# Attention ahead of two mixture layers: float32 matmuls on halves and quarters of the array in place of split operands

## The chip, the core and the metric

One NeuronCore of one Trainium2 chip runs the whole program in one launch. The metric is device time in microseconds (us), the median of several runs. In the profile PE is TensorE (matmuls), PEld its weight loads, DVE is VectorE, ACT is ScalarE, POOL is GpSimd and SP issues the DMAs.

## The reference, cut to what matters

```python
B, H, S, D = 4, 8, 576, 64              # q, k, v: (4, 8, 576, 64) float32
q_rot, k_rot = rotate(q), rotate(k)      # rotary embedding over halves of D
scores = D ** -0.5 * q_rot @ k_rot.T     # 576 x 576 for each of 32 heads
scores = scores - max(scores, axis=-1)
attn = exp(scores); attn = attn / (sum(attn, axis=-1) + 1e-09)
x = (attn @ v), heads side by side       # 2304 tokens x 512
x = relu(x @ w_in) ** 2 @ w_out          # 512 -> 2048 -> 512
out = top-1 mixture of 8 experts of x    # 512 -> 1024 -> 512 each, scaled by two gates
```

All inputs are float32, and so is the output.

## The kernel before

The 32 heads are taken in 16 pairs (`NP`), two heads j = 0, 1 in the two halves of the 128 partitions. `prepare(p)` loads q and k of a pair, rotates them (a shuffle on VectorE, two products and a sum on GpSimd) and builds the matmul operands; `unit(P, p, c)` takes 128 queries of the pair (c = 0 to 3; c = 4 takes the last 64 queries of both heads together) through scores, least value, exponential and transposes; `values(P, p, g)` multiplies by v once a group of queries is complete (group 0: 256 queries, group 1: 320). q and k carry the sign and scale so that the search is for a minimum.

The kernel does its matmuls in the type `F32R` (float32r in the program), whose products keep fewer bits than float32. So each operand is split into a high part (a copy rounded to `F32R`) and a low part (the value minus its high part), and products of parts are added up in PSUM. In attention that means: `high_k`/`low_k` (tile `hl`) and `high_q`/`low_q` (tile `d`), with two DMAs a head (`fan`) that put k under both halves; `v_high`/`v_low` (`vh`); and for the exponentials (`pt`), once turned by TensorE into `tp`, a high copy `phi` on ScalarE and a low part `plo` on VectorE (`evacuate`). What is left of a row beyond 512 keys has its own PSUM tile, `rem`. `scores` are 4 matmuls of 128x128 by 288 for a head and 128 queries.

The least score of a row is found by a `tensor_reduce` on VectorE straight from PSUM (`least`, L473); `exponential` (L479) then reads the scores from the same PSUM tile with that least value as its bias.

The order of work on each engine is not written by hand. `Plan` gets every step with its engine, a price in ns, its dependencies, the tile slots that it uses (`Ring`) and a key, runs through them once, and emits them in the order of their planned start; a step of low priority (a high key) fills what the others leave open. Two rings matter here: scores have two PSUM tiles (`ps_s`), transposes two (`ps_t`); `rem` and `ov` (the product with v) have one bank each.

Beside attention, `add_conversion` turns the 64-bit copies of w_in and w_out into pages of high and low parts (16 values of f, two half conversions for each: three steps on ScalarE, L740, L720 and L747, and four on VectorE, L728, L733, L743 and the subtraction `pg<-m,pg`). They have the lowest priority in attention and mostly run in the first block behind it. Behind attention come four blocks of 512 tokens and one of 256 through the first layer (L841 and L871), then routing and the experts; these are not touched by the change but for the numbers of the planner.

A step `warm` at the start has TensorE do 24 `F32R` matmuls and some float32 ones on zeros, on half the rows (64*128) and quarters (64*64) of the array, while the first loads run (L280, L283, L292). Its results are not used.

Of the kernel before, what the change touches and what calls it, by code (L numbers as in the profile page):

```python
# [28 lines left out]
HB = S // 2  # L29
GRP = ((0, 256), (256, 320))  # L30
# [3 lines left out]
NF0, NF1 = 2, 4  # L34
# [9 lines left out]
ROPE, SPLIT, TURN, SHIFT = "pppppp", "aapppp", "aaaaaaaaaaaa", "aaaa"  # L44


TAIL, LATE = -25204, -2110543
HI, LO = "aaavaaav", "vpvvvpvv"
DMA_RATE = 241
AHEAD = dict(ACT=225, DVE=15, PE=4, POOL=207, SP=534)  # L50
BEGIN = (4, 6, 6, 1)
SECOND = "ap"
EXPONENT = "a"
KEYS = dict(fan=-1072502, swap=10791310, step=11801431, conv=17070875, x0=6215731, end=10978483, load=-22393304, rope=15947290, qk=10250273, v=2755321, s=-18767946, min=-13921801, exp=2252693, rc=-16180141, t=8460321, hi=331733, lo=-7898202, pv=15728628, x=-132386)
# [143 lines left out]
def two_moe_kernel(ctx, tc, qk, v, tab, cst, w_in, w_out, wg, w1, w2, out):  # L198
# [51 lines left out]
    def add_attention(ctx, rest, first):  # L250
# [4 lines left out]
        ps_1 = pool(ctx, "ps_1", 1, space=PSUM)  # L255
# [3 lines left out]
        tabs = pre.tile([128, 4, S], F32, name="tabs")  # L259
        ring_x, ring_hl, ring_d = plan.ring(2), plan.ring(2), plan.ring(2)  # L260
        ring_vr, ring_vh, ring_xt = plan.ring(1), plan.ring(2), plan.ring(2)
        ring_s, ring_p, ring_t = plan.ring(2), plan.ring(3), plan.ring(2)
        ring_rem, ring_o = plan.ring(1), plan.ring(1)
        ring_h = [plan.ring(1), plan.ring(1)]
        ring_sm, ring_f = plan.ring(2), plan.ring(1)
        sums = [big.tile([128, 9], F32, name=f"sums{i}") for i in range(2)]

        ends_q = big.tile([128, 2, 128], F32R, name="dz")
        ring_z = plan.ring(1)
        zeros = [plan.add("DVE", 150, lambda: ve.memset(f32(ends_q), 0.0), -5000000, [], [])]  # L270
        ready = plan.add("SP", 780, lambda: sp.dma_start(out=ident, in_=cst[:, 0:128]), -5000000, [], [])

        def warm():
            z = ends_q.rearrange("p j q -> p (j q)")
            y = f32(z)
            t = [ps_1.tile([128, 512], F32, tag=t, name=n) for t, n in (("o", "ov"), ("rem", "rem"))]
            half = slice(0, 64), slice(64, 128)

            def rows(h, x, m=128, c=0):
                te.matmul(out=t[h][c:c + m, 0:256], lhsT=x[half[h], 0:m], rhs=x[half[h]], start=True, stop=True)  # L280

            def turn(h, i):
                te.transpose(out=t[h][:, 64 * i:64 * i + 64], in_=y[half[h], 0:128], identity=ident[half[h], half[h]])  # L283

            def quads(x, n):
                for i in range(n):
                    for c in (0, 64):
                        for h in range(2):
                            rows(h, x, 64, c)

            for i in range(24):
                te.matmul(out=t[i % 2][:, 0:256], lhsT=z[:, 0:128], rhs=z, start=True, stop=True)  # L292
            quads(y, 4)
            for i in range(3):
                for h in range(2):
                    rows(h, y)
            for i in range(4):
                for h in range(2):
                    turn(h, i)
            quads(y, 1)  # L300
            for i in range(4):
                for h in range(2):
                    turn(h, i)
            quads(y, 1)

        plan.add("PE", 10000, warm, -5000000, zeros + [ready], [ring_o.take(), ring_rem.take()])

        def prepare(p):
# [4 lines left out]
            xs = ring_x.take()  # L313

            first = p == 0

            def load(i):

                if "x" not in T:
                    T["x"] = pre.tile([128, 4, S], F32, tag="x", name="x", bufs=2)  # L320
                sp.dma_start(out=T["x"][:, 2 * i], in_=qk[p, :, i])
                if first and i:
                    sp.dma_start(out=tabs[:, 2:4], in_=tab)

            def swap(i):
                ve.stream_shuffle(out=T["x"][:, 2 * i + 1], in_=T["x"][:, 2 * i], mask=[j ^ 1 for j in range(32)])  # L326

            def mul(i):
                x = T["x"]
                eng(3 * (i // 2) + i % 2).tensor_tensor(out=x[:, i], in0=x[:, i], in1=tabs[:, i], op=ALU.mult)  # L330

            def add(i):
                x = T["x"]
                eng(3 * i + 2).tensor_tensor(out=x[:, 2 * i], in0=x[:, 2 * i], in1=x[:, 2 * i + 1], op=ALU.add)

            def operand():
                if "d" not in T:
                    T["d"] = two.tile([128, 2, 3, S], F32R, tag="d", name="d")
                return T["d"]

            def high_k():
                T["hl"] = pre.tile([128, 2, S], F32R, tag="hl", name="hl", bufs=2)
                copy(split[1], T["hl"][:, 0], T["x"][:, 2])

            def low_k():
                sub(ve if split[3] == "v" else po, T["hl"][:, 1], T["x"][:, 2], f32(T["hl"][:, 0]))

            def high_q(j, on):
                h = slice(64 * j, 64 * j + 64)
                copy(on, operand()[h, j, 0], T["x"][h, 0])  # L350

            def low_q(j, on):
                h, o = slice(64 * j, 64 * j + 64), slice(64 - 64 * j, 128 - 64 * j)
                sub(ve if on == "v" else po, T["d"][o, j, 0], T["x"][h, 0], f32(T["d"][h, j, 0]))

            def first_high(j, u):
                h, o = slice(64 * j, 64 * j + 64), slice(64 * u, 64 * u + 64)
                se.copy(out=operand()[o, j, 1], in_=T["x"][h, 2])

            def first_low(j, u):  # L360
                h, o = slice(64 * j, 64 * j + 64), slice(64 * u, 64 * u + 64)
                sub(ve, operand()[o, j, 2], T["x"][h, 2], f32(T["d"][h, j, 1]))

            def fan(j):
                h = slice(64 * j, 64 * j + 64)
                for u in (0, 64):
                    sp.dma_start(out=f32(operand()[u:u + 64, j, 1:3]), in_=f32(T["hl"][h]))

            def scale_tables():

                se.activation(out=tabs[:, 0:2], in_=tabs[:, 2:4], func=AF.Copy, scale=-(D ** -0.5))

            on, split = ("vvvvvv", "aavvap") if first else (choice(ROPE, p, 6), choice(SPLIT, p, 6))
            eng = lambda i: ve if on[i] == "v" else po
            price = lambda i: ("DVE", dves(S)) if on[i] == "v" else ("POOL", pool2(S))
            hls, ds = ring_hl.take(), ring_d.take()
            parts = {}
            for i in (1, 0):
                k = key + KEYS["rope"] - i
# [265 lines left out]
        for p in range(NP):  # L645
            P = made.pop(p)
            for c in range(5):
                unit(P, p, c)
# [958 lines left out]
def _shape_constants():  # L1607
# [12 lines left out]
    o = 384  # L1620
# [46 lines left out]
```

## Time and profile before

| | |
|---|---|
| median of 3 runs | 981.05 us (978.38 to 981.15) |
| the profiled execution | 981.04 us, of which 979.3 us are its span |
| PE busy | 934.5 us (95%), 5640 matmuls |
| DVE busy | 662.6 us (68%), 1255 instructions |
| ACT busy | 544.0 us (56%), 1141 instructions |
| POOL busy | 356.9 us (36%), 291 instructions |
| first matmul of the first layer | at 302.2 us |
| clock of TensorE in the span (granted, mean) | 0.985 |

Busy shares are means over stages that differ. Up to some 300 us the program is in attention, and PE, DVE, ACT and POOL are all busy; from there on PE alone is busy nearly throughout. A matmul's busy time includes its way through the array, so that several that follow each other overlap; from the start of one row to the start of the next is what it takes of its engine.

### The profile page before, as it was taken

What the parts mean: (1) busy time and instruction counts of PE and PEld (TensorE: products, weight loads), DVE (VectorE), ACT (ScalarE), POOL (GpSimd) and SP (SyncE); (2) the same over time, 40 slices, a digit from 0 to 9 for tenths busy, and PEclk for the clock granted to TensorE, in tenths of its full rate; (3) what the DMA queues carried; (4) which work ended last, traced back from release to release, by engine and by line L of the source; (5) the groups of instructions that cost most, each with busy time, mean ns of one, the idle gap of its engine ahead of it and who ended that gap; (6) DMA issues with size and microseconds to landing.
All of it is one profiled execution on the core that took longest, in us unless ns stands there. A gap on an engine that the chain in (4) does not pass through costs nothing.

```text
span 979.3 us, 16392 instructions
## 1 busy us (share of the span) xinstructions
PE 934.5 (95%) x5640; PEld 817.6 (83%) x5640; DVE 662.6 (68%) x1255; ACT 544.0 (56%) x1141; POOL 356.9 (36%) x291
## 2 busy tenths in 40 slices
PE   5999999999999999999999999999999899999994
PEld 4898998998897887778777877888998799999993
DVE  7888889899997987542454244353668799367660
ACT  3899999999997786322222223223443464344441
POOL 4899998899962000000000000000131454234440
PEclk8999999999999999999999999999999899999998
DMA  3656874757675661410030002001641512443430
GB/s 119 154 154 178 205 203 132 198 153 205 177 211 178 220 213 54 129 44 1 20 118 26 1 24 74 1 0 34 249 150 45 203 55 78 159 136 136 140 121 18
DMA packets 55704, 115.41 MB, mean 118 GB/s; under 512 B 8992, under 2 KB 18736, under 8 KB 55600
## 3 DMA queue, kind: packets, MB, share of 16 engines
q1 hardware_dynamic: 52480, 104.17, 35.8%
q0 software_dynamic: 3120, 9.96, 3.0%
q8 instruction: 51, 0.84, 0.4%
q14 instruction: 53, 0.43, 0.1%
HBM read 94.24 MB, written 19.21 MB: 116 GB/s over the span
## 4 chain that ended last, share of the span: by engine, by line
PE 64%; DVE 12%; DMA 10%; ACT 7%; POOL 3%; issue 3%; SPq 1%; DVEq 0%; POOLq 0%; ACTq 0%
PE h L841 19%; PE a L871 18%; PE h L1359 8%; PE a L1447 7%; DMA out_dram<-y,sidx 4%; PE sc L458 3%; ACT pt L479 3%; DVE mx L473 3%; PE ov L614 2%; DVE plo L212 2%; PE tp L513 2%; ACT phi L209 2%; DMA pg<-w_dram 1%; DMA x<-qk_dram 1%; DVE x L326 1%
## 5 line engine op out<-in xcount | busy, mean ns | idle before, releaser
L841 PE MATMUL h<-xhi,pg 128*128 128x512 f32 (+1 forms) x640 | 198.9, 374 | 0.0
L871 PE MATMUL a<-gh,pg 128*128 128x512 f32 (+1 forms) x640 | 196.1, 373 | 0.0
L1313 POOL DMA_INDIRECT raw<-x1d,gidx x20 | 20.0, 1000 | 376.7 <-DVE ssc L243 358.2
L848 ACT ACTIVATE r<-h 128x512 f32<-128x512 f32 (+1 forms) x80 | 44.3, 554 | 193.4 <-PE h L841 180.8
L841 PEld LDWEIGHTS h<-xhi,pg 128*128 128x128 f32 x640 | 117.4, 188 | 23.1
L871 PEld LDWEIGHTS a<-gh,pg 128*128 128x128 f32 x640 | 117.2, 188 | 22.1
L856 DVE TENSOR_TENSOR r<-r 128x512 f32<-128x512 f32 (+1 forms) x64 | 40.0, 625 | 124.3 <-ACT gh L852 124.2
L871 PE MATMUL a<-gl,pg 128*128 128x512 f32 (+1 forms) x320 | 119.5, 373 | 1.9 <-DVE gl L212 1.6
L841 PE MATMUL h<-xlo,pg 128*128 128x512 f32 (+1 forms) x320 | 119.0, 372 | 0.0
L473 DVE TENSOR_REDUCE mx<-sc 128x1 f32<-128x576 f32 x144 | 107.1, 750 | 15.3 <-PE sc L458 10.6
L458 PE MATMUL sc<-d 128*128 128x288 f32 x512 | 98.7, 317 | 14.0 <-DVE d L212 10.4
L479 ACT ACTIVATE pt<-sc,mx 128x576 f32<-128x576 f32 x144 | 107.5, 748 | 5.7 <-DVE mx L473 5.1
L1359 PE MATMUL h<-raw,pg 128*128 128x256 f32 x864 | 106.0, 283 | 1.1 <-DVE ht L1368 1.1
L1359 PEld LDWEIGHTS h<-raw,pg 128*128 128x128 f32 x864 | 105.0, 191 | 2.2 <-PE m L911 1.0
L212 DVE TENSOR_TENSOR plo<-tp,phi 128x512 fp32r<-128x512 f32 x144 | 96.3, 682 | 10.8 <-ACT phi L209 9.5
L458 PEld LDWEIGHTS sc<-d 128*128 128x128 f32 x512 | 74.7, 194 | 20.4 <-DVE d L212 11.2
L513 PE MATMUL tp<-ident,pt 128*128 128x128 f32 x576 | 86.2, 275 | 5.0 <-DVE plo L212 4.2
L330 POOL TENSOR_TENSOR x<-x,tabs 128x576 f32<-128x576 f32 x60 | 86.4, 1457 | 7.6 <-DVE x L326 7.3
L209 ACT CAST phi<-tp 128x512 fp32r<-128x512 f32 x144 | 83.1, 586 | 7.3 <-PE tp L513 5.8
L212 DVE TENSOR_TENSOR pg<-pg,pg 128x512 fp32r<-128x512 f32 x90 | 76.0, 872 | 4.3 <-ACT pg L209 4.1
L513 PEld LDWEIGHTS tp<-ident,pt 128*128 128x128 f32 x576 | 68.4, 141 | 7.9 <-issue 2.9
L871 PEld LDWEIGHTS a<-gl,pg 128*128 128x128 f32 x320 | 60.3, 188 | 15.2 <-DVE gl L212 4.5
(236 smaller groups left out, 1743.9 us busy)
## 6 DMA issues: line engine op xcount, KB each, us to landing
pg<-w_dram SPq DMA_DIRECT2D x160, 256.0 KB
d<-hl SPq DMA_DIRECT2D x60, 288.0 KB
x<-qk_dram SPq DMA_DIRECT2D x32, 288.0 KB
xtd<-xt SPq DMA_DIRECT2D x32, 288.0 KB
raw<-w_in_dram SPq DMA_DIRECT2D x16, 512.0 KB
raw<-w_out_dram SPq DMA_DIRECT2D x16, 512.0 KB
vr<-v_dram SPq DMA_DIRECT2D x16, 352.0 KB
x1d<-b SPq DMA_DIRECT2D x18, 256.0 KB
```

The lines of the kernel that those rows point to most:

```text
L209: (ve.tensor_copy if on == "v" else se.copy)(out=out, in_=in_)
L212: eng.tensor_tensor(out=out, in0=a, in1=b, op=ALU.subtract)
L330: eng(3 * (i // 2) + i % 2).tensor_tensor(out=x[:, i], in0=x[:, i], in1=tabs[:, i], op=ALU.mult)
L458: te.matmul(out=t[:, hf, 0:HB], lhsT=ends_q[:, 1] if both else d[:, j, 0, q0 + 64 * j:q0 + 64 * j + n], rhs=d[:, 1 if both else j, part, z ...
L473: ve.tensor_reduce(out=T["mx", j], in_=T["s", j][:, :, 0:HB], axis=AX.XY, op=ALU.min)
L479: se.activation(out=T["pt"][:, j].rearrange("p (a b) -> p a b", a=2), in_=T["s", j][:, :, 0:HB], func=AF.Exp, bias=T["mx", j], scale=-1.0, ...
L513: te.transpose(out=t[:, k], in_=T["pt"][:, j, i:i + 128], identity=ident)
L841: te.matmul(out=G["t"], lhsT=a[:, 128 * c:128 * c + 128], rhs=m[:, c, :n], start=c == 0 and i == 0, stop=c == KC - 1 and i == 2,)
L848: se.activation(out=G["r"], in_=G["t"], func=AF.Relu)
L871: te.matmul(out=T["acc", d][:, :n], lhsT=a[:, 128 * d:128 * d + 128], rhs=m, start=f == 0 and i == 0, stop=f == NF - 1 and i == 2,)
L1359: te.matmul(out=T["t"][:, f], lhsT=m[:, z], rhs=r[:, c], start=i == 0, stop=i == 11)
L1447: te.matmul(out=T["t"], lhsT=a[:, k, 128 * i:128 * i + 128], rhs=m, start=k == 0 and y == 0, stop=k == KF - 1 and y == 2,)
```

## The change

Attention's matmuls run in float32 itself, and nothing in attention is split. One head has 64 rows (D), so a score matmul takes half the array: the two row halves h = 0, 1 multiply at the same time, one for each half of the keys, and write two PSUM banks. k is laid out for this on the host; q of each head is needed in both halves, which two DMAs for a pair (`cross`, tile `c`) provide. The product with v takes quarters of the array (64*64), four at a time; transposes take halves (64*128). When the last step was in quarters, scores are done in quarters as well (`mode`). The exponentials are laid out in blocks of 32 keys of the two heads, so that a turned block of 64 rows holds both.

The least value now comes from a `tensor_scalar` (times 1, minimum into `accum_out`) that also writes the scores to SBUF (`sb`); the exponential reads them there. Turned exponentials are copied once (`pp`), by VectorE or ScalarE as `TURN` says (640 columns on VectorE and 512 on ScalarE for each 128 queries). Transposes, the product with v and the turned sums share two PSUM tiles of two banks (`tp`). The step `warm` is gone; the first pair's rotation stays on VectorE. More pages are placed so that they can be written during attention (`NF0`, `NF1`), and the planner's keys, lookaheads and prices are new. The layer behind attention and the experts have the same instructions, in nearly the same order.

```diff
-NF0, NF1 = 2, 4
+NF0, NF1 = 7, 8
...
-ROPE, SPLIT, TURN, SHIFT = "pppppp", "aapppp", "aaaaaaaaaaaa", "aaaa"
+ROPE, TURN, SHIFT = "pppppp", "vavavavaavav", "aa"
...
-        plan.add("PE", 10000, warm, -5000000, zeros + [ready], [ring_o.take(), ring_rem.take()])
...
+        ring_s, ring_p, ring_t = plan.ring(2), plan.ring(2), plan.ring(2)
+        ring_l, ring_h = plan.ring(3), [plan.ring(1), plan.ring(1)]
...
+        def bank(T):
+            if "t" not in T:
+                T["t"] = ps_t.tile([128, 2, 512], F32, tag="t", name="tp")
+            return T["t"]
...
+            def cross():
+                T["c"] = two.tile([128, S], F32, tag="c", name="c")
+                for h in range(2):
+                    sp.dma_start(out=T["c"][half[h]], in_=T["x"][half[1 - h], 0])
...
+                    mode[0] |= both
+                    for z in half if mode[0] else [slice(0, 128)]:
+                        y, q = (z.start // 64, slice(q0, q0 + 64)) if both else (j, slice(q0 + z.start, q0 + z.stop))
+                        for h in range(2):
                             te.matmul(
-                                out=t[:, hf, 0:HB], lhsT=ends_q[:, 1] if both else d[:, j, 0, q0 + 64 * j:q0 + 64 * j + n],
-                                rhs=d[:, 1 if both else j, part, z], start=part == 1, stop=part == 2 and not both,
+                                out=t[z, h, 0:HB], lhsT=(x[half[h], 0] if h == y else P["c"][half[h]])[:, q],
+                                rhs=x[half[h], 1, HB * y:HB * y + HB], start=True, stop=True,
                             )
...
-                    ve.tensor_reduce(out=T["mx", j], in_=T["s", j][:, :, 0:HB], axis=AX.XY, op=ALU.min)
+                    T["sc", j] = two.tile([128, 2, HB], F32, tag="sc", name="sb", bufs=3)
+                    ve.tensor_scalar(
+                        out=T["sc", j], in0=T["s", j][:, :, 0:HB], scalar1=1.0, scalar2=None, op0=ALU.mult, op1=ALU.min,
+                        accum_out=T["mx", j],
+                    )
...
+                        in_=T["sc", j].rearrange("p h (k r) -> p h k r", r=32),
                         func=AF.Exp, bias=T["mx", j], scale=-1.0, accum_out=sums[p % 2][:, i:i + 1],
...
-                P.setdefault(("lows", g), []).append(plan.add("DVE", dve(cols), lo, key + KEYS["lo"], [a], slots + [hs]))
...
+                for i in range(nk):
+                    for h in range(2):
+                        z = 128 * (k0 + i) + (0 if both and h else 64)
+                        te.transpose(
+                            out=t[:, h, 64 * i:64 * i + 64], in_=T["p"][half[h], z:z + 128], identity=ident[half[h], half[h]]
+                        )
...
+                for k in range(k0, k1, 2):
+                    for c in range(2):
+                        z = slice(0, gn) if k + 1 < NK else slice(m * c, m * c + m)
+                        kc = min(k + c, NK - 1)
+                        for j in range(2):
+                            te.matmul(
+                                out=t[half[c], j, z], lhsT=P["v"][half[j], kc], rhs=P["pt", g][half[j], kc, z],
+                                start=k == 0, stop=k + 1 == NK,
+                            )
```

On DVE in a later pair of attention, the kernel before (`sc` scores, `mx` the least value, `tp` and `rem` turned exponentials, `phi` and `plo` their parts, `sums` the pair's sums):

```order
L572 RECIPROCAL sums_120<-sums_120 128x9
L212 TENSOR_TENSOR plo<-tp,phi 128x4x128
L473 TENSOR_REDUCE mx<-sc 128x1
L212 TENSOR_TENSOR plo<-tp,phi 128x4x128
L212 TENSOR_TENSOR plo<-rem,phi 128x384
L733 SCALAR_TENSOR_TENSOR b<-m,b 128x512
L473 TENSOR_REDUCE mx<-sc 128x1
L212 TENSOR_TENSOR plo<-tp,phi 128x8x64
L212 TENSOR_TENSOR plo<-tp,phi 128x4x128
L473 TENSOR_REDUCE mx<-sc 128x1
```

And the same place of the changed kernel (`sb` the scores in SBUF, `pp` the copied exponentials, `w` the shuffled q or k, `pg` a page's low part):

```order
L441 RECIPROCAL sums_116<-sums_116 128x9
L300 STREAM_SHUFFLE w<-x 128x576
L212 COPY pp<-tp 128x2x5x64
L371 TENSOR_SCALAR sb,mx<-sc 128x576 x2
L212 COPY pp<-tp 64x4x64 x2
L371 TENSOR_SCALAR sb,mx<-sc 128x576 x2
L212 COPY pp<-tp 128x2x5x64
L371 TENSOR_SCALAR sb,mx<-sc 128x576 x2
L215 TENSOR_TENSOR pg_3_3704<-m,pg_2_3448 128x512
L212 COPY pp<-tp 128x2x5x64
L371 TENSOR_SCALAR sb,mx<-sc 128x576
```

Between two reciprocals, that is for a pair, there stand 9 searches in both; the 11 subtractions are gone (9 of 512 columns, one of 384 and one of 256), and 4 copies of 640 and 2 of 256 columns stand there instead. Of the four VectorE steps of a half conversion two stand in a pair, so every pair holds half of one.

On PE in a pair, the kernel before (`ov` is the product with v):

```order
L458 MATMUL sc<-d 128x288 x4
L513 MATMUL tp<-ident,pt 128x128 x4
L518 MATMUL rem<-ident,pt 128x128
L458 MATMUL sc<-d,dz 128x288 x2
L466 MATMUL sc<-d,dz 128x64 x2
L466 MATMUL sc<-d,dz 128x224 x2
L458 MATMUL sc<-d,dz 128x288 x2
L466 MATMUL sc<-d,dz 128x288 x2
L513 MATMUL tp<-ident,pt 128x128 x4
L614 MATMUL ov<-plo,vh 128x256 x4
L619 MATMUL ov<-plo,vh 128x256
```

And the changed kernel (`64x` rows are quarters of the array):

```order
L406 MATMUL tp<-ident,pt 128x64 x10
L363 MATMUL sc<-x,c 128x288
L363 MATMUL sc<-x 128x288
L363 MATMUL sc<-x 64x288
L363 MATMUL sc<-x,c 64x288 x2
L363 MATMUL sc<-x 64x288
L406 MATMUL tp<-ident,pt 128x64 x26
L363 MATMUL sc<-x 128x288
L363 MATMUL sc<-x,c 128x288
L481 MATMUL tp<-pp,v 64x256 x16
L481 MATMUL tp<-pp,v 64x128 x4
```

Scores of 128 queries are two matmuls in place of four, the last 64 queries four in place of ten, and the product with v of a group is 20 matmuls on quarters in place of two passes with high and low parts; where it stands among the scores and transposes hardly moves.

## Rows read from the trace of the kernel before

**Rows 1.** Busy time by stretch: late attention, then the first layer's first block.

```profile
211.00:298.00 87.00, 82.42 (x631) 77.88 (x629) 81.60 (x136) 84.78 (x203) 76.14 (x63) 1.00 0.73 193
310.00:390.00 80.00, 80.00 (x351) 65.20 (x351) 66.27 (x116) 63.52 (x111) 0.00 (x0) 1.00 0.53 170
```

**Rows 2.** One line's instructions: start of a pair's reciprocals, first and last.

```profile
L570 ACT ACTIVATE sums<-sums x16: 212/212/216, 39.7 to 298.0; 128x9 f32<-128x9 f32 x16
```

**Rows 3.** High copies of w_in and w_out pages before 300 us.

```profile
L747 ACT CAST pg<-m x7: 603/624/646, 140.0 to 288.2; 128x512 fp32r<-128x512 f32 x7
```

**Rows 4.** PE in order of time in `warm`: start, duration, shape.

```profile
6.47 0.38 PE L280 MATMUL ov<-dz 64*64 64x256 f32 x1
...
6.69 0.38 PE L280 MATMUL ov<-dz 64*64 64x256 f32 x1
...
8.63 0.38 PE L280 MATMUL ov<-dz 64*128 64x256 f32 x1
...
8.85 0.38 PE L280 MATMUL ov<-dz 64*128 64x256 f32 x1
...
9.40 0.22 PE L283 MATMUL ov<-ident,dz 64*128 64x64 f32 x1
...
9.46 0.22 PE L283 MATMUL ov<-ident,dz 64*128 64x64 f32 x1
...
9.62 0.43 PE L280 MATMUL ov<-dz 64*64 64x256 f32 x1
```

**Rows 5.** DVE in order of time in attention.

```profile
200.08 0.81 DVE L326 STREAM_SHUFFLE x<-x 128x576 f32<-128x576 f32 x1
200.79 0.74 DVE L473 TENSOR_REDUCE mx<-sc 128x1 f32<-128x576 f32 x1
201.45 1.27 DVE L212 TENSOR_TENSOR plo<-tp,phi 128x512 fp32r<-128x512 f32 x2
202.64 0.74 DVE L473 TENSOR_REDUCE mx<-sc 128x1 f32<-128x576 f32 x1
```

**Rows 6.** DVE's conversion groups, 100 to 272.2 us: busy, mean ns.

```profile
L728 DVE TENSOR_SCALAR b<-m 128x512 int32<-128x512 int32 x6 | 5.5, 923 | 0.1
...
L212 DVE TENSOR_TENSOR pg<-m,pg 128x512 fp32r<-128x512 f32 x4 | 5.5, 1366 | 0.0
L733 DVE SCALAR_TENSOR_TENSOR b<-m,b 128x512 int32<-128x512 int32 x6 | 5.2, 869 | 0.0
L743 DVE CUSTOM_DVE_ANT_0 m<-b,s 128x1024 uint16<-128x1024 uint16 x6 | 5.0, 828 | 0.0
```

**Rows 7.** ACT in order of time in attention.

```profile
199.79 0.59 ACT L209 CAST phi<-tp 128x512 fp32r<-128x512 f32 x1
200.27 0.75 ACT L479 ACTIVATE pt<-sc,mx 128x576 f32<-128x576 f32 x1
200.91 0.20 ACT L479 ACTIVATION_READ_ACCUMULATOR pt<-sc,mx 128x1 f32 x1
201.00 0.59 ACT L209 CAST phi<-tp 128x512 fp32r<-128x512 f32 x1
```

**Rows 8.** ACT's groups, 100 to 272.2 us: a cast that reads SBUF.

```profile
L209 ACT CAST hl<-x 128x576 fp32r<-128x576 f32 x10 | 6.8, 676 | 0.0
```

**Rows 9.** POOL's groups, 100 to 272.2 us: products of the rotation.

```profile
L330 POOL TENSOR_TENSOR x<-x,tabs 128x576 f32<-128x576 f32 x39 | 56.3, 1459 | 4.0 <-DVE x L326 3.8
```

**Rows 10.** First load, and what waited for it and the tables.

```profile
0.73 0.40 SPq L321 DMA_DIRECT2D x<-qk_dram  x1
...
3.61 0.01 DVE L326 LOAD_MASK_SELECT x<-x  x1 [2.48 <-DMA x<-qk_dram]
...
5.49 1.43 DVE L330 TENSOR_TENSOR x<-x,tabs 128x576 f32<-128x576 f32 x2 [1.08 <-DMA tabs<-tab_dram]
```

**Rows 11.** PE's busy time and granted clock, in `warm` and behind it.

```profile
9.50:11.20 1.70, 1.70 (x30) 1.00 0.10 26
11.20:18.00 6.80, 0.06 (x4) 0.81 0.16 53
```

More of the change, by code (lines that the diff above doesn't have):

```diff
@@ L264, in add_attention @@
[L264 to L304, printed above, removed]
@@ L312, in prepare, with order, load_table @@
             key = 50 * p
-            xs = ring_x.take()
-            first = p == 0
+            xs, ws, cs, vs = ring_x.take(), ring_w.take(), ring_c.take(), ring_v.take()
+            start = p == 0
+            def order(name, more=0):
+                return (HEAD[name] if start else key + KEYS[name]) + more
+            def load_table(i):
+                z = slice(S * i, S * i + S - i * HB)
+                sp.dma_start(out=tabs[:, :, z], in_=tab[:, :, z])
             def load(i):
                 if "x" not in T:
[L320 to L323, printed above, removed]
+                    T["x"] = two.tile([128, 2, S], F32, tag="x", name="x", bufs=3)
+                sp.dma_start(out=T["x"][:, i], in_=qk[p, :, i])
@@ L439, in prepare @@
+            if start:
+                fanned.append(T["q"])
+            T["cross"] = plan.add("SP", 1220, cross, order("fan"), [T["q"]], [xs, cs])
+            T["vl"] = plan.add("SP", 1220, load_v, key + KEYS["load"], fanned, [vs])
+            T["slots"] = xs, cs, vs, ring_sm.take()
+            prepared.extend([T["k"], T["q"]])
+            begin.append([T["cross"]])
             return T
@@ L490, in unit @@
-                ends.append(plan.add("ACT", 730, exponential, key + KEYS["exp"], [b] + ends, [ss, ps_, sms]))
-                scored.append(ends[-1])
+                a = plan.add("PE", 560 if both else 490, scores, key + KEYS["s"], [P["q"], P["k"], P["cross"]], [ss, xs, cs])
+                ls = ring_l.take()
+                b = plan.add("DVE", 760, least, key + KEYS["min"], [a], [ss, ls])
+                ends.append(plan.add("ACT", 770, exponential, key + KEYS["exp"], [b] + ends + zeros, [ls, ps_, sms]))
@@ new lines, in values, with out @@
+            on = choice(SHIFT, p, 2)[g]
+            def out():
+                if "xt" not in P:
+                    P["xt"] = big.tile([128, 2, S], F32, tag="xt", name="xt", bufs=2)
+                copy(on, P["xt"][:, :, g0:g0 + gn], R["t"][:, :, 0:gn])
+            m = None
+            for k0, k1 in PV:
+                m = plan.add(
+                    "PE", 0.85 * (min(k1, NK) - k0) * gn + 150 * (not k0), lambda k0=k0, k1=k1: product(k0, k1),
+                    key + KEYS["pv"], [m] if m else P["his", g] + [P["vl"]], [ts, hs, vs],
+                )
```

325 lines of the change are left out of this document (104 added, 221 removed).

## Prediction

> **What bounds the kernel now.** I read the busy shares by stretch first. Late in attention, 211 to 298 us, PE, DVE, ACT and POOL are busy for 82.42, 81.60, 84.78 and 76.14 of 87 us [rows 1]: three engines share the bound, and POOL is not far off. In the first layer's first block behind it PE is busy for 80.00 of 80 us while DVE has 66.27 and ACT 63.52. So the time is attention, set by several engines at once, and then a long stage that PE alone sets and that the change leaves as it is. A microsecond taken from attention comes off the end, if the block behind it finds its weights.
>
> Next, how long a pair takes. One ACT instruction marks the end of each pair: it first starts at 39.7 us and last, the 16th time, at 298.0 us [rows 2]. That is (298.0 - 39.7) / 15 = 17.22 us for a pair, and 39.7 us up to the end of the first one. The sum below is made of these two numbers.
>
> Then what attention gives to the stage behind it: by 300 us 7 of the 32 high copies of pages have run [rows 3], so 25 half conversions fall into the first block, which still keeps PE busy.
>
> **The change, part by part.** A pair has 9 searches (8 of 128 queries and one of the last 64 of both heads).
>
> PE. The step `warm` runs the new forms, so their prices are rows of before. A float32 matmul is two instructions there. Quarters, 256 columns: four at a time start 6.69 - 6.47 = 0.22 us after the four before them [rows 4], so four matmuls take 0.43 us. Halves, 256 columns: 8.85 - 8.63 = 0.22, so two matmuls take 0.43 us, 1.68 ns a column. Two transposes of 64 columns take 9.46 - 9.40 = 0.06 us. Going from transposes to quarters takes 9.62 - 9.46 = 0.16, so 0.1 more. A pair: 8 scores of two halves by 288, 8 x 0.48 = 3.9; the last queries on quarters 0.48; 45 pairs of transposes, 2.8; v, 4.5 groups of four quarters by 256 and by 320, 4.5 x (0.43 + 0.54) = 4.4; some six changes of shape 0.6. Sum 12.1 us.
>
> DVE. It loses the 11 subtractions, at (202.64 - 201.45) / 2 = 0.60 us for 512 columns [rows 5]. It keeps 9 searches, two shuffles (200.79 - 200.08 = 0.71 each), a reciprocal (0.2) and half a half conversion. The search was 201.45 - 200.79 = 0.66 us for 576 columns from PSUM. The new one reads the same columns, also writes them, and has an accumulator output; no row of VectorE shows one. Lower bound 0.66. Upper bound: ACT's read of its accumulator, 0.20 us long, added whole, 0.86. I take 0.76, since on ACT that read moves the next instruction by only 201.00 - 200.91 = 0.09 us [rows 7]. By the Trainium skill (VectorE: DVE Perf Modes, section on two Vector instructions with no wait between them) an operation that writes out its accumulator is two instructions; no run here shows it for VectorE, and the page has no price. New are the copies: 0.60 us for 512 columns from PSUM and 0.66 for 576 give about 0.73 for 640 and 0.33 for 256, so 4 x 0.73 + 2 x 0.33 = 3.6. The four steps of a half conversion have means of 0.92, 0.87, 0.83 and 1.37 us in attention [rows 6], 4.0 together; the last of these is twice what the same 512-column subtraction from PSUM takes, so it waits while GpSimd works. Half of it is 2.0 at most, 1.2 if GpSimd, less busy now, lets it through; I take 1.7. Sum: 9 x 0.76 + 3.6 + 1.4 + 0.2 + 1.7 = 13.7 us; bounds 12.3 (0.66 and 1.2) and 14.9 (0.86 and 2.0).
>
> ACT. An exponential takes 201.00 - 200.27 = 0.73 us from PSUM, and a cast of 512 columns 200.27 - 199.79 = 0.48. The exponential now reads SBUF. A cast from SBUF of 576 columns is 0.68 us long [rows 8]; 512 columns from PSUM are 0.59, which is 0.64 at 576, so 0.04 more: 0.77. A pair: 9 x 0.77 = 6.9; four copies of 512 columns 1.9 and two of 320, 0.6; the product with v out of PSUM in two copies of 512 and 640, 1.1; sums 0.3; three conversion steps at about 0.5, half of them 0.8. Sum 11.6 us; the nine high copies, the casts of q and k are gone.
>
> POOL. Left are six products and sums at 1.46 us [rows 9], 8.8 us. It drops out of the bound; what covers it is the 13.7 us of DVE, and with the rotation two pairs ahead nothing waits for it.
>
> DMA. `fan` goes, two transfers for a pair (`cross`) come. At some 2.9 us (a first load is issued at 0.73 and waited for until 3.61 [rows 10]) they lie beside the pair ahead; only in the first pair are they on the path.
>
> So DVE becomes the longest, with PE at 88% and ACT at 85% of it. The busiest engine of before reached 84.78 / 87 = 97%. The lookahead on the tiles is about the same (two for scores, two for transposes and products), and three engines pass work back and forth in a fixed order, so I take 96%: 13.7 / 0.96 = 14.3 us for a pair, against 17.22. That gives 15 x 2.92 = 43.8 us.
>
> The first pair. Before it ends at 39.7 us. After: tables at 5.49 [rows 10], then DVE's four products and two sums at about 0.72 and a shuffle, 5.0, so 10.5; `cross` 2.9, so 13.4; then a pair's work without conversion, 12.0, with four more shuffles, 2.8, the routing's constants, which I put at 2.7, and 1 us for the way out: 32 us. That is 8 us less; bounds 4 and 12. `warm` costs nothing now, since the loads and rotation hide it; its removal gains nothing.
>
> The stage behind. In the changed order 7 high copies stand ahead of the first matmul of the first layer, as many as ran before it until now, so the block finds its pages as before; what covers the rest is DVE's room there, 80 - 66 = 14 us. The transposes and products that end attention lie among that block's matmuls in both. I take nothing for it. Moves among routing and experts are few: nothing, within 3 us either way.
>
> Sum: 981.04 - 43.8 - 8 = 929.2 us. The profiled execution (981.04) is at the median of the runs shown (981.05), so 929 us is also the forecast for the median.
>
> **Rivals.**
>
> *TensorE's clock falls in attention (slower).* All the new matmuls use halves or quarters of the array, and a quarter of PE's work is transposes. At 1.2 GHz PE would need 2 x 12.1 = 24.2 us a pair: 981 + 15 x (24.2 - 17.22) - 8 = 1078 us. It decides as soon as a pair exceeds 17.22 + 8 / 15 = 17.75 us, that is, with PE at the lower level for (17.75 - 12.1) / 12.1 = 47% of its work. Against it: `warm` ran such matmuls and transposes from 6 to 11 us, the stretch 9.50 to 11.20 still has a granted 1.00, and the fall (0.81 as a mean) comes in 11.20 to 18.00, where PE has nothing to do [rows 11]. But that is a short test, and it followed full-array matmuls. The Trainium skill (TensorE: Matmul & The Clock Gate, Part 4) says that transposes do not count as PE-busy in the same way, which is this rival; the trace of before has more transposes a pair, and a granted 1.00 [rows 1].
>
> *DVE is dearer.* At 14.9 us a pair and 94% (DVE's own share late in attention), 15.9: 981 - 15 x 1.3 - 8 = 953 us. The same would come of the shared `tp` tiles: two serve 13 users a pair, and a product holds one for 3 us and more.
>
> *DVE is cheaper, PE binds.* The search at 0.66 and the conversions at 1.2 give 12.3; PE's 12.1 then counts as well, and with both at 94% a pair takes 13.0: 981 - 63 - 10 = 908 us.
>
> *The change does nothing*, as the tiles' ring holds a pair at 17 us: its 13 users would have to hold a tile for 2 x 17.2 / 13 = 2.6 us each. A transposing user needs 0.3 on PE and 0.7 in the copy, and about 1.5 with the hand-overs: unlikely.
>
> **How the numbers follow.** Forecast 0.59 (a pair at 13.5 to 15.2, 914 to 944 us), DVE dearer 0.17, PE binding 0.16, clock 0.04, no change 0.02, a first block starved of weights or other losses beyond 0.3% 0.02. The range takes in the forecast and the two cases about it, 904 to 956 us; clock, no change and the tails are left out. About 0.3% is what a measurement of this kernel can tell from no change. Faster by more than that 0.92 (the forecast and the two cases about it), within it 0.02, slower 0.06.
>
> **What would show it.** In the profile after: the pair's mark (the same activation of the sums) some 14.3 us apart, the first near 32 us; DVE busy for over 90% of a late stretch, PE and ACT below it; the search at 0.76 us from start to start; granted clock 1.00 from 30 us on; the first layer's first matmul near 250 us, and PE busy throughout behind it. It is wrong if the clock reads less than 1.00 in attention, if PE waits for `tp` tiles, or if the first block waits for pages.

## The result, and the profile after

The changed kernel takes 938.5 us (median of 4 runs, 937.3 to 940.0) against 981.1 us on the same chip (4 runs, 978.4 to 981.3): a ratio of 0.957, 95% interval 0.955 to 0.960. The forecast was 929 us, with 904 to 956 as its range. The profiled execution has a span of 938.2 us, 41.1 less than before.

The same mark as in [rows 2], the activation of a pair's sums (line and engine, its durations in ns, first and last start):

```profile
L439 ACT ACTIVATE sums<-sums x16: 211/212/213, 30.6 to 259.7; 128x9 f32<-128x9 f32 x16
```

And the first layer's first matmul, from the same view of its line (302.2 us before):

```profile
L720 PE MATMUL h<-xhi,pg x640: 274/392/502, 260.1 to 686.0; 128*128 128x512 f32 x128, 128*128 128x256 f32 x32
```

So a pair takes (259.7 - 30.6) / 15 = 15.27 us instead of 17.22, the first pair ends at 30.6 instead of 39.7, and the first layer starts 0.4 us behind the last mark instead of 4.2. The books: first pair -9.1, fifteen pairs -29.2, hand-over to the first layer -3.8, everything behind it +1.0: -41.1 us.

Busy time by stretch, three from attention and the first block (columns as in [rows 1]):

```profile
60.00:120.00 60.00, 55.49 (x848) 34.47 (x846) 54.61 (x125) 50.35 (x120) 34.73 (x25) 1.00 0.46 137
120.00:180.00 60.00, 55.34 (x846) 34.39 (x840) 53.23 (x124) 49.79 (x118) 34.89 (x25) 1.00 0.45 137
180.00:240.00 60.00, 55.37 (x848) 34.38 (x846) 51.91 (x122) 50.81 (x120) 31.29 (x22) 1.00 0.59 171
260.00:340.00 80.00, 80.00 (x401) 63.58 (x396) 68.45 (x119) 66.65 (x117) 0.00 (x0) 1.00 0.56 183
```

Before, three engines were busy for 94 to 97% of late attention [rows 1]. Now no engine is: PE has 92% (with the modelled ends of its matmuls), VectorE 89%, ScalarE 84%. The clock reads 1.00 in these stretches, and the first block still keeps PE busy for all of its 80 us.

Ahead of them it did not always: PE waits 2.8 us for a copy on ScalarE, up to 31.35 us, and then runs at a lower clock until 40 us (the last column but two):

```profile
28.00:32.00 4.00, 1.08 (x24) 0.79 (x22) 3.99 (x14) 1.70 (x5) 2.34 (x3) 1.00 0.51 125
32.00:36.00 4.00, 3.47 (x30) 2.13 (x32) 3.50 (x9) 2.32 (x6) 3.92 (x3) 0.68 0.58 217
36.00:40.00 4.00, 3.96 (x42) 2.23 (x42) 3.52 (x8) 3.41 (x8) 3.92 (x4) 0.90 0.02 4
```

The second and the third mark come 17.29 and 16.40 us behind the mark before them; from there (64.30) to the fifteenth (245.14) a pair takes 15.07 us. So 15.27 is a mean with a slow start in it. How much of the first 17.29 us the clock costs is not told apart.

Where the time of a pair goes is told by the chain of work that ended last, over 60 to 240 us, as shares by line:

```profile
by line: PE tp L481 32.7%; PE sc L363 19.7%; PE tp L406 17.3%; ACT pt L380 13.2%; ACT pp L212 12.8%; issue 3.1%; PE tp L447 1.4%
```

The reader should see what is missing: VectorE, forecast as the longest engine, has no piece of it. The chain goes through PE for 71% of the time and through ScalarE (an exponential, then a copy out of a `tp` tile) for 26%, back and forth. PE's own waits there, over 12 pairs (engine, line, who released it, sum, times, longest):

```profile
PE tp L406 <- ACT pt L380: 7.6, 12, 0.8
PE tp L406 <- ACT pp L212: 4.6, 12, 0.4
PE tp L481 <- ACT pp L212: 1.0, 6, 0.2
```

Once a pair PE's transposes wait for an exponential, and once for a copy out of a `tp` tile. Scores do not stand among PE's waits.

The search, 60 to 240 us (groups of instructions; busy us, mean ns of one, idle before):

```profile
L371 DVE TENSOR_SCALAR_CACHE_REDUCE sb<-sc 128x576 f32<-128x576 f32 x108 | 78.9, 752 | 0.7
L212 DVE COPY pp<-tp 128x640 f32<-128x640 f32 (+1 forms) x72 | 49.4, 686 | 17.4 <-PE tp L406 17.0
...
L371 DVE DVE_READ_ACCUMULATOR sb<-sc 128x1 f32 x108 | 9.0, 83 | 0.0
```

and two searches in a row on VectorE's timeline (start, length):

```profile
183.20 0.75 DVE L371 TENSOR_SCALAR_CACHE_REDUCE sb<-sc 128x576 f32<-128x576 f32 x1
183.87 0.08 DVE L371 DVE_READ_ACCUMULATOR sb<-sc 128x1 f32 x1
183.87 0.75 DVE L371 TENSOR_SCALAR_CACHE_REDUCE sb<-sc 128x576 f32<-128x576 f32 x1
184.55 0.08 DVE L371 DVE_READ_ACCUMULATOR sb<-sc 128x1 f32 x1
```

From start to start a search takes 0.67 us, as the plain reduction did (0.66 in [rows 5]). The accumulator read is there, 83 ns long, and lies beside the start of the next instruction: the copy of the scores costs VectorE next to nothing (0.67 instead of 0.66 us).

### The profile page after: what moved, and what is told of

It reads as the page before. It is cut to its first block, busy times and chain, and to the rows that moved or that the text cites. A ratio compares the mean times of both kernels' runs of the same rounds, so it can differ in the third digit from the quotient of the medians.

```text
span 938.2 us, 18525 instructions
## 1 busy us (share of the span) xinstructions
PE 884.2 (94%) x6916; PEld 696.4 (74%) x6916; DVE 622.1 (66%) x1312; ACT 477.4 (51%) x974; POOL 247.1 (26%) x187
## 3 DMA queue, kind: packets, MB, share of 16 engines
q1 hardware_dynamic: 50640, 90.44, 30.6%
## 4 chain that ended last, share of the span: by engine, by line
PE 78%; DMA 7%; ACT 7%; DVE 5%; issue 2%; SPq 0%; POOL 0%; POOLq 0%; DVEq 0%; ACTq 0%
PE h L720 21%; PE a L750 20%; PE h L1238 9%; PE tp L481 8%; PE a L1326 8%; PE sc L363 5%; DMA out_dram<-y,sidx 5%; PE tp L406 4%; ACT pt L380 3%; ACT pp L212 3%; PE m L827 1%; PE m L1206 1%; PE m L790 1%; DMA raw<-x1d,gidx 1%; DVE xlo L215 1%
## 5 line engine op out<-in xcount | busy, mean ns | idle before, releaser
L380 ACT ACTIVATE pt<-sb,mx 128x576 f32<-128x576 f32 x144 | 111.1, 773 | 6.7 <-DVE sb L371 6.2
L363 PE MATMUL sc<-x 64*128 64x288 f32 (+1 forms) x320 | 100.1, 445 | 11.2 <-DVE x L310 10.7
L371 DVE TENSOR_SCALAR_CACHE_REDUCE sb<-sc 128x576 f32<-128x576 f32 x144 | 105.4, 752 | 7.4 <-PE sc L363 6.3
L363 PE MATMUL sc<-x,c 64*128 64x288 f32 (+1 forms) x320 | 99.3, 446 | 2.6 <-DMA c<-x 1.7
L406 PEld LDWEIGHTS tp<-ident,pt 64*128 64x128 f32 x1440 | 56.3, 139 | 49.1 <-ACT pt L380 16.2
L406 PE MATMUL tp<-ident,pt 64*128 64x64 f32 x1440 | 68.4, 230 | 19.5 <-ACT pt L380 9.2
L215 DVE TENSOR_TENSOR pg<-pg,pg 128x512 fp32r<-128x512 f32 x90 | 82.7, 946 | 5.8 <-ACT pg L212 5.6
L481 PE MATMUL tp<-pp,v 64*64 64x320 f32 (+3 forms) x1280 | 80.3, 386 | 1.7 <-ACT pp L212 1.0
L212 DVE COPY pp<-tp 128x640 f32<-128x640 f32 (+1 forms) x96 | 65.8, 686 | 21.3 <-PE tp L406 20.6
L481 PEld LDWEIGHTS tp<-pp,v 64*64 64x64 f32 x1280 | 44.6, 132 | 34.1 <-DVE pp L212 9.1
```

The source lines that it names most:

```text
L212: (ve.tensor_copy if on == "v" else se.copy)(out=out, in_=in_)
L215: eng.tensor_tensor(out=out, in0=a, in1=b, op=ALU.subtract)
L363: te.matmul(out=t[z, h, 0:HB], lhsT=(x[half[h], 0] if h == y else P["c"][half[h]])[:, q], rhs=x[half[h], 1, HB * y:HB * y + HB], start=Tru ...
L371: ve.tensor_scalar(out=T["sc", j], in0=T["s", j][:, :, 0:HB], scalar1=1.0, scalar2=None, op0=ALU.mult, op1=ALU.min, accum_out=T["mx", j],)
L380: se.activation(out=T["p"][:, 64:].rearrange("p (k j h r) -> p j h k r", j=2, h=2, r=32)[:, j], in_=T["sc", j].rearrange("p h (k r) -> p h ...
L406: te.transpose(out=t[:, h, 64 * i:64 * i + 64], in_=T["p"][half[h], z:z + 128], identity=ident[half[h], half[h]])
```

## Experiments

Three theories for a pair of 15.27 us. **A**: a chain of hand-overs between PE, ScalarE and VectorE over two score tiles and two `tp` tiles. **B**: VectorE's work, as predicted. **C**: PE's work alone. In the experiments the mark of [rows 2] is read, as first and last start; a pair is a fifteenth of what lies between. The planner makes a new order whenever a price or a ring changes, so an experiment that changes one of these changes the order too; in the last four the order is chosen anew. A mark can also move among a pair's work: in run 5 the marks come 15.05 and 20.35 us apart in turn, with 8 and 10 searches between them. So only means over many pairs are compared. Ratios are to the kernel before on the same chip, which took 977.5 to 979.4 us beside these runs.

**1. The search as a plain reduction.**

```diff
-ve.tensor_scalar(out=T["sc", j], in0=T["s", j][:, :, 0:HB], scalar1=1.0, ..., op0=ALU.mult, op1=ALU.min, accum_out=T["mx", j])
+ve.tensor_reduce(out=T["mx", j], in_=T["s", j][:, :, 0:HB], axis=AX.XY, op=ALU.min)
...
-in_=T["sc", j].rearrange("p h (k r) -> p h k r", r=32),
+in_=T["s", j][:, :, 0:HB].rearrange("p h (k r) -> p h k r", r=32),
```

> The changed kernel with the search for the least score as a plain reduction again; the exponential reads the scores from PSUM and so holds their tile until its end. A: a pair of 15.27 us is a chain of hand-overs between PE, VectorE and ScalarE over few tiles: PE then waits for score tiles, a pair grows by 0.3 to 1.0 us, total 943 to 954 us. B: VectorE's work sets the pair, as predicted: the search takes 0.66 to 0.68 us in both forms, so the pair stays, 936 to 941 us. C: PE's work alone sets it: the same, 936 to 941.

996.9 us, 1.020 of the kernel before (1.018 to 1.022): the whole gain is lost, and more. The marks go from 33.3 to 316.2 us, 18.86 us a pair. B and C said no change and fall here in their plain form; A had the sign and far too small a size. Two things lie over each other in it, which the stretches show:

```profile
60.00:120.00 60.00, 46.52 (x664) 29.96 (x664) 57.20 (x89) 47.64 (x108) 30.30 (x20) 0.91 0.52 153
120.00:180.00 60.00, 46.62 (x662) 30.05 (x664) 56.42 (x89) 46.28 (x107) 29.32 (x20) 0.91 0.51 152
180.00:240.00 60.00, 46.70 (x724) 30.00 (x720) 47.00 (x75) 41.78 (x99) 31.30 (x22) 1.00 0.40 114
```

Up to 180 us VectorE is busy for 94 to 95% (the new order puts more conversions there) and the clock is granted at 0.91; behind that neither holds, and it is still slow.

**2. Conversions held back until the last pair.**

```diff
-weights = [add_conversion(..., begin[BEGIN[min(f, 3)]], ...) ...]
+weights = [add_conversion(..., begin[NP - 1], ...) ...]
```

> The changed kernel with the loads of all weight conversions held back until the last pair, so that in attention VectorE loses some 1.8 us of its 13.3 us a pair and ScalarE 0.8 us. B (VectorE sets the pair): a pair falls from 15.27 us to 13.2 to 13.8 us, attention ends 22 to 31 us earlier. A (hand-overs): less than 0.5 us a pair, attention ends less than 8 us earlier. C (PE): nothing, attention ends where it did. The first block of the first layer then has to hold all conversions and waits for pages in each case, so the total says little; the end of the last pair (259.7 us) is what counts.

The marks: 30.6 to 257.4 us, 15.12 a pair, 2.3 us less in all. VectorE is busy for only 80% now, ScalarE for 78%, PE for 93%, as before:

```profile
120.00:180.00 60.00, 55.53 (x858) 34.57 (x856) 47.72 (x117) 47.04 (x114) 33.41 (x24) 1.00 0.41 121
```

That is A's and C's number, and B falls: VectorE's work goes from 89% of 15.27 us to 80% of 15.12, some 1.5 us a pair, and 0.15 comes off. Not even that is sure to be the conversions' doing: in run 7, where they stay, a pair takes 15.15 (30.2 to 257.4). The total is 955.3 us (0.978, 0.974 to 0.982), with the first block now having PE busy for only 68.89 of its 80 us from 260 on: so conversions in attention's gaps are worth their place.

**3. Less PE work.** Of the product with v, the groups k = 2 and 6 are left out.

```diff
 for k in range(k0, k1, 2):
+    if k in (2, 6):
+        continue
```

> The changed kernel without two of the four full groups of keys in the product with v (k = 2 and 6 are left out, so that part of the output's sum is missing), in a plan with the same prices. PE loses some 1.95 us of its 13.1 us a pair, and each product holds its tile about 1 us less; VectorE and ScalarE lose nothing. B (VectorE sets the pair): 15.2 us still, total 936 to 941 us. C (PE): 13.3 us a pair, total near 909 us. A (hand-overs): between them, 13.7 to 14.7 us, total 915 to 930 us.

The marks: 30.5 to 242.9 us, 14.16 a pair, 1.1 us of the 1.95 that PE lost by the estimate from `warm`; A's range. (The total, 931.1 us, isn't compared: other values route tokens to other experts.) VectorE was busy for 95% there, so B could still claim the rest; the sixth run tests that.

**4 and 8. Tiles shifted between scores and transposes.** Three `tp` tiles and one for scores; then one and three.

```diff
-ps_t = pool(ctx, "ps_t", 2, space=PSUM)
-ps_s = pool(first, "ps_s", 2, space=PSUM, side="right")
+ps_t = pool(ctx, "ps_t", 3, space=PSUM)
+ps_s = pool(first, "ps_s", 1, space=PSUM, side="right")
...
```

The planner's rings follow. With three and one, the pool `ps_m` of a later stage also opens later, behind attention.

> The changed kernel with three tiles for transposes and products and one for scores, instead of two and two; no engine's work changes. A, if the tiles tp are what is short: a pair falls by 0.5 us or more, total below 931 us. A, if the tiles for scores are as short: a pair grows, total above 945 us. B and C (the work of one engine sets the pair): 15.0 to 15.5 us, 935 to 942 us.

> The mirror of the fourth experiment: three tiles for scores, one for transposes and products. A (few tiles, hand-overs): a pair grows to 20 us or more, total above 1010 us, since a product and a transposing user can no longer overlap. B and C (an engine's own work): 15 to 15.5 us.

Three and one: 1031.0 us (1.053, 1.049 to 1.057), marks 34.8 to 358.9, 21.6 us a pair. One and three: 1075.1 us (one run), marks 30.6 to 398.6, 24.5 a pair. No engine's instructions differ from the changed kernel's. The waits from 60 to 240 us are those of the tile that was taken away: in the first, PE's scores wait 30.0 us for searches that free their tile; in the second, its transposes wait 41.9 us for copies out of theirs. Both kinds of tile are short, as A says, and neither has one to spare. The sizes hold more than that: in 60 to 120 us the clock reads 0.74 in the one and 0.81 in the other.

**5. The first and the second together**, to take the conversions out of the first.

> The reduction kernel of the first experiment, with the conversions' loads also held back until the last pair, as in the second; the second (15.12 us a pair, attention's end at 257.4 us) is what it is compared with. If the first experiment lost its time because the exponential holds the score tile (A): 17 us a pair or more, attention's end beyond 285 us, PE waiting for exponentials. If it lost it because the planner put conversions into VectorE's gaps in a bad place, or because VectorE is the bound (B): about 15.2 us a pair, end near 259 us.

The marks: 33.5 to 305.7 us, 18.15 a pair, against 15.12 with the copying search. The stretch, and PE's waits over 60 to 240 us:

```profile
120.00:180.00 60.00, 47.98 (x754) 31.15 (x752) 40.26 (x68) 39.73 (x97) 24.95 (x18) 1.00 0.40 113
```

```profile
PE tp L401 <- ACT pt L376: 21.2, 16, 1.6
PE sc L363 <- ACT pt L376: 14.5, 10, 1.5
PE tp L476 <- DVE pp L212: 4.7, 10, 0.6
```

The clock is 1.00, VectorE is busy for 67%, ScalarE for 66%, PE for 80%: no engine is near full, and a pair takes 3 us longer. The second wait is the one that the copying search removes: PE's next scores wait until the exponential has read the tile. It is some 1.5 us a pair itself (ten pairs in this stretch); transposes that wait for exponentials are another 2.1, against 0.9 in run 2. Conversions and clock are not all that made the first run slow (A, not B); what part the order has, run 9 tells.

**6. The third and the second together**: less work on PE, VectorE and ScalarE.

> Two of the four full groups of keys are left out of the product with v, as in the third experiment (14.16 us a pair), and the conversions are held back as well, so that PE, VectorE and ScalarE all have less to do. If PE's work is the main bound (C): the whole 1.95 us comes off, 13.0 to 13.3 us a pair, attention's end near 227 us. If it is hand-overs that less work does not shorten (A): 13.6 to 14.1 us a pair. If VectorE was what stopped the third experiment at 14.16: below 13.6.

The marks: 30.8 to 244.2 us, 14.23 a pair, not less than in the third.

```profile
120.00:180.00 60.00, 51.51 (x776) 31.29 (x772) 51.84 (x127) 49.97 (x122) 38.05 (x28) 1.00 0.43 128
```

PE is at 86%, VectorE at 86%, ScalarE at 83%, all with less to do than in the changed kernel, and of the 1.95 us that PE lost 0.9 does not come off (15.27 - 14.23 = 1.04). This is against C and against VectorE as what stopped the third run; it lies a little above A's range (13.6 to 14.1) as a mean. Most pairs take 13.8; the mean has in it the first interval (16.67) and one of 16.23, in which the clock was granted at 0.89.

**7. A step like `warm` again**, 30 float32 matmuls on zeros ahead of the first scores.

```diff
+def warm():
+    t = bank({})
+    for i in range(30):
+        te.matmul(out=t[:, i % 2, 0:128], lhsT=sums[0], rhs=sums[0], start=True, stop=True)
+plan.add("PE", 7000, warm, -5000000, zeros, [ring_t.take()])
```

> The changed kernel with 30 float32 matmuls on zeros ahead of the first pair's scores (a step like warm, full array, results unused); the order of everything else stays. If the removal of warm cost nothing, as predicted: first pair's end at 30.3 to 30.8 us (30.6 without it), total unchanged. If the first pair's scores ran slowly because the array had done nothing before: the step from one score to the next falls from 0.96 us to about 0.5 us between 14.8 and 18.7 us, and the first pair ends 0.5 to 2 us earlier; the total moves by less than can be told.

937.1 us, 0.958 (0.954 to 0.962): the same. The first pair ends at 30.2 instead of 30.6, and the early scores keep their pace up to 17.9 us. Removing `warm` cost 0.4 us at most, where the forecast had nothing.

**9. The plain reduction with an order of its own.** As the first, with the planner's prices set to measured ones, and keys, lookaheads and `TURN` chosen anew (`TURN` "vavavaaaavav").

> The reduction kernel again (plain search, exponential reads PSUM and holds the score tile), this time with keys, lookaheads and the engines of the copies chosen anew for it, and the planner's prices set to the measured ones, so that the order suits it. If only the order was bad in the first and fifth experiments (the copying search itself being worth nothing): 15.3 us a pair, total 936 to 944 us. If the hold of the score tile costs time in any order (A): 16.2 to 17.6 us a pair, total 952 to 975 us.

960.8 us, 0.982 (0.978 to 0.985); marks 31.8 to 280.7, 16.59 a pair, in A's range. So 2.3 of the first run's 3.6 us a pair were the order, which had been made for the copying search (with the clock of 0.91 that came with it), and 1.3 us remain in an order made for the reduction. Not all of the 1.3 need be the hold of the tile, since this order fills VectorE with conversions up to 180 us:

```profile
120.00:180.00 60.00, 50.15 (x790) 33.17 (x788) 59.39 (x100) 56.30 (x127) 36.15 (x24) 1.00 0.57 174
180.00:240.00 60.00, 52.39 (x818) 33.97 (x816) 44.87 (x78) 48.07 (x113) 30.89 (x23) 1.00 0.43 124
```

Behind that VectorE has room, and a pair still takes 15.95 us (four pairs, 183.3 to 247.0) against 15.05 at the same place of the changed kernel (185.0 to 245.1): 0.9 us that neither a full VectorE nor the clock explains. The wait of run 5 is there too (60 to 240 us):

```profile
PE sc L363 <- ACT pt L376: 8.3, 12, 0.8
```

**10 and 11. The changed kernel in another order**, chosen in the same way, then also with `warm`.

```diff
-ROPE, TURN, SHIFT = "pppppp", "vavavavaavav", "aa"
+ROPE, TURN, SHIFT = "pppppp", "aaaavvvaavav", "av"
...
-AHEAD = dict(ACT=188, DVE=29, PE=82, POOL=2353, SP=1548)
+AHEAD = dict(ACT=22, DVE=92, PE=74, POOL=192, SP=1211)
...
```

The keys and the planner's prices change as well.

> The changed kernel, all its steps kept, with keys, lookaheads and the engines of copies chosen anew, and the planner's prices set to the measured ones (scores 520 and 640 ns, search 680, transposes 20 + 66 a block). A: order and hand-overs set the pair, so another order may move it: 14.6 to 15.1 us a pair, total 925 to 936 us. B or C: the engines' work is the same, 15.2 us, within 0.3% of 938.5 us.

> As the one before, with the 30 matmuls on zeros of the seventh experiment at the start: 0.4 us less up to the end of the first pair, as there; the total the same within what can be told.

932.2 us, 0.952 (0.949 to 0.955), and 933.3 us, 0.953 (0.950 to 0.957). The marks of the first: 27.0 to 256.5 us, 15.30 a pair. A had said 14.6 to 15.1, so its expectation missed by this count. But the early first mark is no gain: the second comes at 48.8 us, 0.9 later than in the changed kernel (47.9). From the second mark to the last a pair takes 14.84 here and 15.13 there, and that is where the 3.2 us up to the last mark come from. The other 3.1 us lie behind it; the first layer's first matmul runs at 253.0 us, before the last mark. Also, VectorE does more in attention and is nearly full:

```profile
120.00:180.00 60.00, 56.65 (x868) 36.31 (x868) 59.43 (x134) 53.27 (x125) 36.98 (x24) 1.00 0.55 161
```

VectorE is busy for 99% here; in the first block it has 57 us of 80 instead of 68. So at some 15 us a pair several limits lie close together, and in this order VectorE is near its own. Against the changed kernel the gain is 0.5% by ratios whose intervals just touch. With `warm` the first mark is at 27.2: no gain this time.

**12. The copying search alone**, in the kernel before. Keys and lookaheads are chosen anew, and one page set less is placed for attention, since the copies need its room.

> The kernel before with only the copying search added (the exponential reads the copy, the score tile is free after the search), keys and lookaheads chosen anew for it, and one page set less placed for attention, since the copies take its room. If the copying search is a gain by itself because it frees score tiles (A): 16.4 to 16.9 us a pair, total 965 to 975 us. If before was bound by its engines (ScalarE 97% busy late in attention) and not by tiles: 17.2 us or more a pair, since ScalarE's read from SBUF costs it 9 x 0.04 us, total 977 to 990 us.

968.4 us, 0.990 (0.987 to 0.993); marks 39.8 to 287.9, 16.54 a pair, A's expectation. ScalarE's share stays high (98% from 120 to 180 us), and the pair is shorter all the same; how much of it is the new order is not told apart. The wait that the copy removes was small in the kernel before; PE's scores waited for an exponential (100 to 290 us, some 11 pairs):

```profile
PE sc L458 <- ACT pt L479: 1.6, 3, 0.7
```

That is 0.15 us a pair, less than the 0.7 that came off, so the freed tile is not shown to be the cause here.

The four combinations side by side:

| | pair, us | first mark | total, us | of before |
|---|---|---|---|---|
| before | 17.22 | 39.7 | 981.1 | 1 |
| copying search alone (12, new order) | 16.54 | 39.8 | 968.4 | 0.990 |
| all but the copying search (9, new order) | 16.59 | 31.8 | 960.8 | 0.982 |
| both, the changed kernel | 15.27 | 30.6 | 938.5 | 0.957 |
| both, new order (10) | 15.30 | 27.0 | 932.2 | 0.952 |

Each half of the change takes 0.6 to 0.7 us off a pair, and both together 1.95: more than their sum. As every row has an order of its own, how much of this is the orders is not shown.

## Why the prediction was right, and where its step failed

**Direction and the parts.** Right: three engines lose work, attention gets shorter, the first block keeps PE busy, the clock is at 1.00 from 40 us on, and the first pair is 9.1 us shorter (forecast 8). `cross` lands and the second score starts at 13.70 us (forecast 13.4). VectorE's sum was right: busy for 89% of 15.27 us, 13.5 us, against 13.7. Its parts were off against each other: the search is 0.67, not 0.76 (9 x 0.09 = 0.8 us too much). The Trainium skill (VectorE: DVE Perf Modes, section on two Vector instructions with no wait between them) has an accumulator output as two instructions. The trace agrees, and adds that the second one, 83 ns, held up nothing: the next search starts with it, at 183.87 us.

**The step that failed** is "DVE becomes the longest ... so I take 96%". That share was carried over from the kernel before, where three engines had it at once. Here a pair is set by the chain from PE to ScalarE and back, VectorE is not in it, and its share comes out as 89%. Taking 1.5 us of VectorE's work out of a pair took 0.15 us off it (run 2). The term was 14.3 us a pair and measured 15.27: 15 x 0.97 = 14.6 us too little, of which 5.1 lie in the two slow intervals behind the first mark. The first pair (9.1 us less instead of 8) gives 1.1 back, and what lies behind the last mark 2.8 (3.8 at the hand-over, less 1.0 later): 929.2 + 14.6 - 1.1 - 2.8 = 939.9, against 940.0 for the profiled execution. That these two came out the other way, by 3.9 us together, is luck: the total is nearer to the forecast than the pair is.

**PE's sum** was too small as well: 12.1 forecast. In a run of PE's timeline without waits

```profile
186.38 0.46 PE L363 MATMUL sc<-x 64*128 64x288 f32 x1
186.38 0.46 PE L363 MATMUL sc<-x,c 64*128 64x288 f32 x1
186.68 0.40 PE L363 MATMUL sc<-x 64*128 64x288 f32 x1
186.68 0.40 PE L363 MATMUL sc<-x,c 64*128 64x288 f32 x1
186.94 0.78 PE L406 MATMUL tp<-ident,pt 64*128 64x64 f32 x18
187.61 0.51 PE L363 MATMUL sc<-x,c 64*128 64x288 f32 x1
```

scores take 186.94 - 186.38 = 0.56 us where 0.48 was worked out, and 18 transposes 187.61 - 186.94 = 0.67 where nine pairs of them, a fifth of 2.8, gave 0.56. With the product with v (183.13 to 185.23 and 191.35 to 194.31 us, 5.1 in place of 4.4) and the last queries at 0.64, PE needs some 13.5 us a pair, as much as VectorE. The prices from `warm` were those of one form repeated, and the work changes form all the time; that this is the reason was not tried.

**The rivals.** The one that came true in part is the half sentence on the shared `tp` tiles (15.9 us a pair); the time came out between it and the forecast, and just outside the forecast's own 13.5 to 15.2. Its mechanism is wider than was put there: score tiles are as short as `tp` tiles (runs 4, 5 and 8). Two of the three signs by which the prediction would be wrong came: "if PE waits for `tp` tiles", which PE does for about 0.4 us a pair, and 0.6 for exponentials; and a clock below 1.00 in attention, from 32 to 40 us. "PE binds" at 13.0 us, "no change" and a starved block did not come. The rival of the clock came for these eight microseconds only, behind a long wait of PE; from 40 us on the clock reads 1.00, with matmuls on halves and quarters alone. The Trainium skill (TensorE: Matmul & The Clock Gate, Part 4) says that transposes do not count as PE-busy in the same way. No run here shows a loss by it: in the changed kernel they are a quarter of PE's work (5 x 0.67 of 13.5 us), at a granted 1.00.

**What the prediction did not see** is what the copying search is for. It was costed as VectorE's work, at 0.1 us more than before, and nothing was put on the other side: that a score tile is free after the search and not after the exponential. Run 5 against run 2 puts 3.0 us a pair on that with keys made for the copying search; run 9 against the changed kernel puts 1.3 us on it in orders made for each, and 0.9 where VectorE has room. The Trainium skill (Perfetto Trace Analysis, Optimizing Tensor Performance) advises to rotate independent matmul groups through PSUM banks, so that emptying one lies beside the next group's matmuls; here freeing a tile earlier served the same end with the same two tiles: from 60 to 240 us PE's scores wait 14.5 us for exponentials in run 5 and not at all in the changed kernel.

**What stays open.** Of a pair's last 1.7 us (13.5 to 15.27) PE's waits are 1.1 (13.7 us over 12 pairs: 7.6 for exponentials, the rest for copies), and the slow start is 0.2; some 0.4 are not accounted for. What makes the kernel of run 12 faster is open as well. A third tile of one kind without losing one of the other wasn't tried.

## What to carry to other kernels

When a change takes the load off several engines at once, don't carry the busy share of before over to the new longest engine: look for the chain through the tiles, count for each tile how long its producer, its readers and the way back hold it, and set that beside the engines' sums. A cheap operation that reads a PSUM tile can copy it as well, and free it for the next matmul before the slow reader has run; its worth shows in the wait of the next matmul, not in its own engine's time, so look first whether that wait is there. And an experiment that undoes one part under a planner needs an order of its own: here the undoing cost 3.6 us a pair in the wrong order and 1.3 in a fitting one. Nor does one early mark prove a gain: run 10 had lost its 3.6 us by the next mark.

## What the runs showed of the hardware that was not expected

The early scores. In the changed kernel the granted clock reads 1.00 from 14 to 18 us, and yet from 16.53 to 17.49 us 0.48 us pass from one pair of a score's matmul instructions to the next (16.53, 17.01, 17.49), where 0.26 to 0.30 is usual later on (186.38, 186.68, 186.94). The same 0.48 comes back at 35.57, 36.05 and 36.53 us, where the granted clock reads 0.68 and 0.90. In run 7 the scores of that time go at the same pace (16.33, 16.82, 17.30), and there the record shows it (the clock is the last column but two):

```profile
14.00:16.00 2.00, 2.00 (x8) 1.08 (x10) 0.93 (x3) 0.28 (x1) 0.00 (x0) 0.61 1.06 358
16.00:18.00 2.00, 2.00 (x10) 0.81 (x9) 1.36 (x4) 1.99 (x4) 0.00 (x0) 0.54 0.95 331
```

So at the start of an execution a granted 1.00 does not prove that the matmuls ran at 2.4 GHz; the spacing of the matmuls does.

The clock with waits in attention. From 60 us on it stayed at 1.00 in the changed kernel (PE busy for 55.4 of 60 us) and in run 5 (45.8 to 48.0), and was granted at 0.91 in run 1 up to 180 us (46.5 and 46.6; 1.00 behind it, with 46.7) and at 0.74 to 0.84 in run 4 up to 180 us and in run 8 (43.6 to 48.5; 0.97 behind it in run 4, with 45.7). Which of their waits made the difference was not tried.
